# A new written order for the first two token blocks of a fused retention and expert kernel

## Chip, cores and metric

The kernel runs on one core of a Trainium2 chip. The metric is the device time of one execution in microseconds (us), as the median of several executions. Times inside an execution come from one profiled execution and are counted from the start of its span.

## What is computed

Decayed causal attention (retention) over 8 sequences of 576 positions with 8 heads of 64, then a dense expert layer with a sigmoid-approximated gelu, then a soft mixture of 8 experts with 4 slots each. All inputs and outputs are float32.

```python
ret = (q @ k.T / sqrt(64)) * gamma[h] ** (i - j)  for i >= j     # 8 x 8 x 576 x 576
x = (ret @ v), heads side by side                                # 4608 x 512
h = x @ w_in                                                     # 4608 x 2048
x = (h * sigmoid(1.702 * h)) @ w_out                             # 4608 x 512
logits = x @ phi                                                 # 4608 x 32
slot_input = softmax(logits, over tokens).T @ x                  # 32 x 512
slot_out[e] = relu(slot_input[e] @ w1[e]) @ w2[e]                # 8 experts, 4 slots each
out = softmax(logits, over slots) @ slot_out                     # 4608 x 512
```

## The kernel before

The 4608 tokens form 12 blocks of 384. A block is three steps of 128 tokens (two sequences at one chunk of 64 positions each), and nine steps make one pass over the sequence for two sequences. A step is loaded by one 1 MB transfer (`load_step`, token T), its keys are scaled on GpSimd (`scale_keys`, KN), and TensorE makes its scores (transposed), its contribution to the running state and its output (`products`, line 220: tiles Sp, St, Op). VectorE scales scores (SC), state (SS) and output (xs) out of PSUM, and the output is split into a high part (ScalarE, `x_high`, xh) and a low part (`x_low`, xl, on VectorE for steps 0 to 2 and on GpSimd from step 3 on).

A block then meets 16 weight chunks of the expert layer. One expert product (`expert_scores`, line 357, token M) is 12 matmuls of 128x384: high by high, high by low, low by high, for four pieces of the inner dimension. They read all 384 columns of the block's high and low part, so no product of a block can pass its second matmul before all three low parts are written. ScalarE makes the gelu (g), VectorE turns it (t), and when eight are turned SP shuffles them to natural order by transfers (N, 16 transfers for half a block).

The weights arrive as 64-bit words, of which the kernel makes float32: ScalarE brings the sign (ua for `w_in`, aa for `w_out` turned), VectorE shifts the low word (us, as) and joins the two (uc, ac). `w_in` is then split into high (ScalarE, h) and low (VectorE, v). Of `w_out` turned, TensorE makes `w_out @ phi` (e, line 326), which VectorE turns into Wp (ed), and the logits of a group of four chunks are products with Wp (L). Raw weights land in seven places that are used in turn (W and O tokens), so a load waits for the join or split of the piece seven before it. `slots_part` (SG, line 468) sums the natural gelus of a block into the slots.

Blocks 0 and 1 (16 + 16 expert products, M0 to M31) stand in a list of tokens, `START`, that is written out by hand. Each engine runs its own instructions in the order of this list, and nothing is reordered. From block 2 on loops write the order. Among the tokens: B0 and B3 are score products alone, P and A are products of a step with output, Q output alone, R state alone (R2: the state products of the third step). D is a product of line 558 on the loaded keys of the pack that step 3 takes over; its result is not used. G is one element on ScalarE that the first weight load waits for, so that the first three steps land ahead of the weights. K loads three small constants.

```python
    def again():
        t = ps.tile([128, NB], F32, tag="h", name="again", bufs=3)
        a = packs[0].rearrange("p c a j d -> p (c a j d)")
        pe.matmul(t, a[:, 0:128], a[:, 0:NB], start=True, stop=True)
```

Of the kernel before, what the change touches and what calls it, by code (L numbers as in the profile page):

```python
# [9 lines left out]
F32 = mybir.dt.float32  # L10
F32R = mybir.dt.float32r
I32 = mybir.dt.int32
AF = mybir.ActivationFunctionType
# [5 lines left out]
B, H, S, D = 8, 8, 576, 64  # L19
# [7 lines left out]
C = 64  # L27
NPB = S // C
NP = H // 2
NB = 384  # L30
# [16 lines left out]
PC = NP * CP  # L47

START = (
# [13 lines left out]
).split()  # L63

RAWS = 7
# [67 lines left out]
def tile_kernel(ctx, tc, qkv, w_in, w_turned, w_out, phi, w1, w2, consts, out):  # L133
    nc = tc.nc
    pe, act, dve, pool, sp = nc.tensor, nc.scalar, nc.vector, nc.gpsimd, nc.sync

    pp = ctx.enter_context(tc.tile_pool(name="pp", bufs=1))
    ps = ctx.enter_context(tc.tile_pool(name="ps", bufs=1, space=PSUM))
# [38 lines left out]
    early_raw = pm.tile([128, 6, 1024], F32, tag="nat", name="early_raw")  # L177
    packs = {g: pa.tile([128, 6, NP, NSEQ, C], F32, name=f"pack{g}", bufs=1) for g in range(2)}
# [6 lines left out]
    St, Sps, Ops, xss = {}, {}, {}, {}  # L185
# [79 lines left out]
    wt = {}  # L265
# [41 lines left out]
    def w_high(fc):  # L307
        if fc in (0, NFC - 1):
            wt[fc] = pw.tile([128, 2, NDC, 128], F32R, tag="w1", name="w", bufs=2)
        elif fc % 2:  # L310
            two = pw.tile([128, 2, 2, NDC, 128], F32R, tag="w", name="w")
            wt[fc], wt[fc + 1] = two[:, 0], two[:, 1]
        act.copy(wt[fc].rearrange("p a c f -> p a (c f)")[:, 0], raws[f"W{fc}"][0].bitcast(F32))

    def w_low(fc):
# [233 lines left out]
    def constants():  # L549
        sp.dma_start(phis.rearrange("p c s -> p (c s)"), phi)  # L550
        sp.dma_start(ident, consts[:, 0:128])
        s4 = st["s4"] = pm.tile([128, 128], F32, tag="dT", name="s4")
        sp.dma_start(s4, consts[:, _CONSTS.shape[1] - 128:])

    def again():
        t = ps.tile([128, NB], F32, tag="h", name="again", bufs=3)
        a = packs[0].rearrange("p c a j d -> p (c a j d)")
        pe.matmul(t, a[:, 0:128], a[:, 0:NB], start=True, stop=True)

    what = {  # L560
        "T": load_step,
        "W": lambda i: load_w(f"W{i}"), "O": lambda i: load_w(f"O{i}"),
        "ua": lambda i: bring_sign(f"W{i}"), "us": lambda i: shift_low(f"W{i}"),
        "uc": lambda i: join(f"W{i}", raws[f"W{i}"][0]), "h": w_high, "v": w_low,
        "aa": lambda i: bring_sign(f"O{i}"), "as": lambda i: shift_low(f"O{i}"),
        "ac": lambda i: join(f"O{i}", ring[:, i % 4]), "e": wp_product, "ed": wp_turn,
# [10 lines left out]
    def step(x):  # L577
        if x == "C":
            sp.dma_start(cs, consts[:, 128:128 + NCS])
        elif x == "K":  # L580
            constants()
        elif x == "D":
            again()
        elif x == "G":
            act.copy(early_raw[0:1, 0, 0:1], St[0][0:1, 0, 0, 0:1])
        elif x == "Z":
            dve.tensor_copy(sum4r, st.pop("s4"))
        else:
            name = x.rstrip("-0123456789")
            what[name](int(x[len(name):]))  # L590
# [230 lines left out]
    with tc.manual_schedule(engines={getattr(mybir.EngineType, e) for e in ("PE", "Activation", "DVE", "Pool", "SP")}):  # L821
        for x in START:
            step(x)
# [122 lines left out]
```

## Time and profile before

| | |
|---|---|
| median of 3 executions | 656.14 us (654.52 to 657.8) |
| the profiled execution, its own time | 653.52 us |
| its span, first to last instruction | 651.7 us |
| TensorE matmul busy in the span | 627.9 us (96%) |
| VectorE, ScalarE, GpSimd busy | 291.7, 218.4 and 80.4 us |
| first expert product of block 0 (M0) begins | 19.59 us |
| first expert product of block 1 (M16), second matmul | 68.87 us |
| first expert product of block 2, second matmul | 119.27 us |

TensorE is busy nearly all the time, so the time of the first two blocks is told by the places where it waits. The last three lines mark the ends of the stages that the change touches; the profiled execution is 2.6 us under the median of the three.

### The profile page before, as it was taken

How to read it: one execution, taken by the hardware profiler on the slowest of the kernel's cores; microseconds unless marked ns; L12 is line 12 of the kernel's file. 1: busy time of each engine (PE TensorE's matmuls, PEld its weight loads, DVE VectorE, ACT ScalarE, POOL GpSimd, SP SyncE). 2: the span in 40 equal slices, each digit the busy share in tenths (PEclk: the TensorE clock that was granted, in tenths of full speed). 3: DMA queues.
4: the chain of work that ended last, by engine and by line, in shares of the span. 5: the costliest groups of instructions: out<-in, count | busy, mean ns of one | idle time of the engine just before them, and what ended most of it. 6: DMA issues, size and time to landing. Idle time of an engine off the chain costs nothing.

```text
span 651.7 us, 19108 instructions
## 1 busy us (share of the span) xinstructions
PE 627.9 (96%) x8439; PEld 540.8 (83%) x8439; DVE 291.7 (45%) x578; ACT 218.4 (34%) x411; POOL 80.4 (12%) x72
## 2 busy tenths in 40 slices
PE   6999999999999999999999999999999999999992
PEld 6898787898989989989989979989898798874562
DVE  3999832364453443444534534544535223122042
ACT  2784432141241332412412412412414224240042
POOL 2103102111112101121111011111111100001000
PEclk9999999999999999999999999999999999999997
DMA  8987657766776647737647557467477778989998
GB/s 341 398 308 285 253 123 204 182 192 163 198 252 171 176 183 191 211 109 200 184 131 206 163 140 215 134 163 199 162 185 200 277 197 244 404 303 419 415 419 345
DMA packets 62546, 150.64 MB, mean 231 GB/s; under 512 B 8192, under 2 KB 42368, under 8 KB 53248
## 3 DMA queue, kind: packets, MB, share of 16 engines
q1 hardware_dynamic: 62464, 149.43, 71.6%
q8 instruction: 66, 1.08, 0.7%
q14 instruction: 16, 0.13, 0.1%
HBM read 101.16 MB, written 13.63 MB: 176 GB/s over the span
## 4 chain that ended last, share of the span: by engine, by line
PE 86%; DVE 5%; DMA 4%; ACT 2%; issue 1%; POOL 0%; SPq 0%; DVEq 0%; ACTq 0%
PE hp L357 56%; PE Lg L408 5%; PE Sg L468 4%; PE Sp L220 4%; PE St L220 4%; PE Op L220 3%; PE h_ps L705 2%; PE op L782 2%; PE so_ps L756 1%; DMA early_raw<-in_moe_w_in_dram 1%; PE so_ps L748 1%; DMA ring<-in_w_turned_dram 1%; DVE w L317 1%; PE tpg L390 1%; DMA pack<-in_qkv_dram 1%
## 5 line engine op out<-in xcount | busy, mean ns | idle before, releaser
L357 PE MATMUL hp<-x,w 128*128 128x384 f32 x2304 | 418.9, 339 | 1.3 <-POOL x L250 1.3
L357 PEld LDWEIGHTS hp<-x,w 128*128 128x128 f32 x2304 | 397.5, 188 | 20.0 <-issue 16.3
L383 DVE STREAM_TRANSPOSE pre<-gT 128x384 f32<-128x384 f32 x172 | 95.1, 568 | 151.0 <-ACT gT L367 149.5
L367 ACT ACTIVATE gT<-hp 128x384 f32<-128x384 f32 x188 | 90.8, 489 | 213.7 <-PE hp L357 213.3
L250 POOL TENSOR_TENSOR x<-xs,x 128x512 fp32r<-128x512 f32 x33 | 42.7, 1293 | 294.5 <-ACT x L245 294.5
L220 PE MATMUL Op<-pack 64*64 64x64 f32 x2176 | 71.9, 220 | 0.2 <-issue 0.2
L220 PEld LDWEIGHTS Op<-pack 64*64 64x64 f32 x2176 | 66.9, 135 | 0.6 <-issue 0.6
L226 POOL TENSOR_TENSOR pack<-pack,cs 128x512 f32<-128x512 f32 x32 | 34.8, 1088 | 142.0 <-DMA pack<-in_qkv_dram 126.1
L245 ACT CAST x<-xs 128x512 fp32r<-128x512 f32 x36 | 22.3, 619 | 85.8 <-DVE xs L238 85.8
L220 PE MATMUL Sp<-pack 64*64 64x64 f32 x1152 | 41.1, 222 | 6.5 <-DMA pack<-in_qkv_dram 6.5
L220 PEld LDWEIGHTS Sp<-pack 64*64 64x64 f32 x1152 | 37.7, 138 | 8.2 <-DMA pack<-in_qkv_dram 5.7
L230 DVE TENSOR_TENSOR pack<-Sp,cs 128x512 f32<-128x512 f32 x36 | 24.8, 688 | 37.8 <-PE Op L220 19.3
L220 PEld LDWEIGHTS St<-pack 64*64 64x64 f32 x1024 | 33.2, 137 | 8.0 <-issue 7.9
L220 PE MATMUL St<-pack 64*64 64x64 f32 x1024 | 37.6, 224 | 0.0
L408 PE MATMUL Lg<-gT,Wp 128*32 128x384 f32 x376 | 36.2, 493 | 0.4 <-DVE Lall L455 0.4
L468 PE MATMUL Sg<-nat,dn 128*32 128x512 f32 x264 | 30.4, 593 | 0.0
L238 DVE TENSOR_TENSOR xs<-Op,cs 128x512 f32<-128x512 f32 x36 | 24.5, 681 | 2.8 <-PE Op L220 2.8
L234 DVE TENSOR_TENSOR pack<-St,cs 128x512 f32<-128x512 f32 x32 | 21.8, 680 | 3.7 <-PE St L220 2.2
L294 ACT ACTIVATE early_raw<-early_raw 128x512 f32<-128x512 f32 x28 | 18.9, 688 | 12.6 <-DMA early_raw<-in_w_turned_dram 7.6
L468 PEld LDWEIGHTS Sg<-nat,dn 128*32 128x32 f32 x264 | 8.5, 110 | 17.0 <-issue 17.0
L294 ACT ACTIVATE ring<-ring 128x512 f32<-128x512 f32 x20 | 13.7, 683 | 23.7 <-DMA ring<-in_moe_w_out_dram 21.3
L474 DVE SCALAR_TENSOR_TENSOR acc<-acc,corr,Sg 128x512 f32<-128x512 f32 x10 | 7.5, 747 | 28.2 <-PE Sg L468 28.2
(143 smaller groups left out, 378.4 us busy)
## 6 DMA issues: line engine op xcount, KB each, us to landing
pack<-in_qkv_dram SPq DMA_DIRECT2D x36, 1024.0 KB, 5.5
nat<-pre SPq DMA_DIRECT2D x352, 96.0 KB, 2.2
wx<-in_moe_w_dram SPq DMA_DIRECT2D x20, 1024.0 KB, 10.9
ring<-in_moe_w_out_dram SPq DMA_DIRECT2D x16, 512.0 KB, 3.7
early_raw<-in_moe_w_in_dram SPq DMA_DIRECT2D x15, 512.0 KB, 5.9
early_raw<-in_w_turned_dram SPq DMA_DIRECT2D x13, 512.0 KB, 7.6
wx<-in_moe_w_dram SPq DMA_DIRECT2D x10, 512.0 KB, 9.1
out_dram<-wx SPq DMA_DIRECT2D x5, 1024.0 KB, 9.1
```

The source lines that it names most:

```text
L220: pe.matmul(o[oh, p, j, :], w[h, a, p, j], w[h, b, p, j], start=first_, stop=True, skip_group_check=True)
L226: pool.tensor_tensor(k, k, by_state(ksc[:, n % NPB, :]), op=ALU.mult)
L230: dve.tensor_tensor(packs[n][:, SC], Sps.pop(n), across(dtab), op=ALU.mult)
L238: dve.tensor_tensor(xss[g], Ops.pop(g), across(osc), op=ALU.mult)
L245: act.copy(xh[b_][:, :, i * CP:(i + 1) * CP], xss[g].rearrange("p a j c -> p a (j c)"))
L250: (eng or pool).tensor_tensor(xl[b_][:, :, cols_], xss.pop(g).rearrange("p a j c -> p a (j c)"), xh[b_][:, :, cols_], op=ALU.subtract)
L294: act.activation(upper, upper, AF.Prelu, scale=2.0 ** -112, alpha=2.0 ** 32)
L357: pe.matmul(hp, wt[fc][:, a, dc, :], b[n][:, dc, :], start=(i == 0), stop=(i == 3 * NDC - 1))
L367: act.activation(gT[n, g][:, fl, :], hps.pop((n, fc)), AF.Gelu_apprx_sigmoid)
L383: dve.transpose(pre[n, hf][:, :, :, fh, :].rearrange("p c b i -> p (c b) i"), gT[n, g][:, fl, :].rearrange("p (x j) -> p x j", j=32))
L408: pe.matmul(Lg[n][32 * fl:32 * fl + 32, :], Wp[:, g * GF + fl, :], gT[n, g][:, fl, :], start=(g == 0), stop=(g == NFC // GF - 1))
L468: pe.matmul(Sg[32 * b:32 * b + 32], dn[n][:, c, :], nv[:, 4 * b:4 * b + 4], start=(c == 0), stop=(c == NT128 - 1))
```

## The change

The list `START` is written anew for all engines. It holds the same tokens, but for the three D, which are gone together with the function `again`. R2 moves ahead of M0. G is now a gelu of one element instead of a copy. `w_high` no longer takes it that the odd one of two chunks comes first. Two lines of the list, of some forty, and the code:

```diff
-    "T0 C T1 T2 B0 KN0 SC0 R0 G SS1 P0 KN1 W0 W1 R1 SC1 T3 W2 xs0 W3 KN2 SS2 P1 xh0 W4 W5 xl0 SC2 T4 ua0 W6 xs1 Q2 D "
+    "T0 C T1 KN0 B0 SC0 R0 SS1 KN1 P0 T2 G SC1 xs0 R1 xh0 W0 P1 W1 K KN2 SS2 ua0 xl0 W2 SC2 us0 Q2 xs1 uc0 xs2 W3 xh1 "
...
-        elif fc % 2:
+        elif fc not in wt:
+            i = (fc - 1) // 2 * 2 + 1
             two = pw.tile([128, 2, 2, NDC, 128], F32R, tag="w", name="w")
-            wt[fc], wt[fc + 1] = two[:, 0], two[:, 1]
+            wt[i], wt[i + 1] = two[:, 0], two[:, 1]
...
-    def again():
-        t = ps.tile([128, NB], F32, tag="h", name="again", bufs=3)
-        a = packs[0].rearrange("p c a j d -> p (c a j d)")
-        pe.matmul(t, a[:, 0:128], a[:, 0:NB], start=True, stop=True)
...
-        elif x == "D":
-            again()
         elif x == "G":
-            act.copy(early_raw[0:1, 0, 0:1], St[0][0:1, 0, 0, 0:1])
+            act.activation(early_raw[0:1, 0, 0:1], St[0][0:1, 0, 0, 0:1], AF.Gelu_apprx_sigmoid)
```

TensorE around the first expert product, before (pack_94 is the third step, pack_92 the first and then the fourth; `again` is D, `hp` an expert product of 12):

```order
L220 MATMUL Op<-pack_94 64x64 x32
L558 MATMUL again<-pack_92 128x384 x3
L357 MATMUL hp<-x,w 128x384 x12
L220 MATMUL St<-pack_94 64x64 x16
L357 MATMUL hp<-x,w 128x384 x24
L220 MATMUL Sp<-pack_92 64x64 x16
L357 MATMUL hp<-x,w 128x384 x48
```

and now:

```order
L220 MATMUL Op<-pack_94 64x64 x32
L220 MATMUL St<-pack_94 64x64 x16
L358 MATMUL hp<-x,w 128x384 x12
L220 MATMUL Sp<-pack_92 64x64 x16
L358 MATMUL hp<-x,w 128x384 x48
```

The state products stand between the outputs of the third step and the first expert product, and the scores of the fourth step follow that product at once; four expert products follow before the next step instead of two and four.

GpSimd ahead of block 2, before (x_1431 is block 2, and xs_1405, xs_1541, xs_1655 are the outputs of steps 6, 7 and 8; pack0_92 holds the keys of step 7 and, in its second row, of step 9):

```order
L226 TENSOR_TENSOR pack0_92<-pack0_92,cs_83 128x512
L250 TENSOR_TENSOR x_1431<-xs_1405,x_1431 128x4x128
L250 TENSOR_TENSOR x_1431<-xs_1541,x_1431 128x4x128
L226 TENSOR_TENSOR pack0_92<-pack0_92,cs_83 128x512
L250 TENSOR_TENSOR x_1431<-xs_1655,x_1431 128x4x128
L226 TENSOR_TENSOR pack1_93<-pack1_93,cs_83 128x512
```

and now (x_1359 is block 2; xs_1353, xs_1531 and xs_1650 are steps 6, 7 and 8):

```order
L226 TENSOR_TENSOR pack0_92<-pack0_92,cs_83 128x512
L250 TENSOR_TENSOR x_1359<-xs_1353,x_1359 128x4x128
L250 TENSOR_TENSOR x_1359<-xs_1650,x_1359 128x4x128
L226 TENSOR_TENSOR pack0_92<-pack0_92,cs_83 128x512
L250 TENSOR_TENSOR x_1359<-xs_1531,x_1359 128x4x128
L226 TENSOR_TENSOR pack1_93<-pack1_93,cs_83 128x512
```

The low part of step 8 now stands ahead of that of step 7, with the keys of step 9 between them.

TensorE at the end of block 1, before (Lg are the logits groups L4 and L5, hp x36 is M28 to M30, Sg is SG0, and with the Sp row the products of step 8, A8, begin):

```order
L220 MATMUL Op<-pack_92 64x64 x2
L408 MATMUL Lg<-gT,Wp 32x384 x8
L357 MATMUL hp<-x,w 128x384 x36
L468 MATMUL Sg<-nat,dn 32x512 x12
L220 MATMUL Sp<-pack_92 64x64 x2
L220 MATMUL Op<-pack_93 64x64 x2
```

and now (M28, SG0, M29, then A8):

```order
L220 MATMUL Op<-pack_92 64x64 x2
L358 MATMUL hp<-x,w 128x384 x12
L469 MATMUL Sg<-nat,dn 32x512 x12
L358 MATMUL hp<-x,w 128x384 x12
L220 MATMUL Sp<-pack_92 64x64 x2
L220 MATMUL Op<-pack_93 64x64 x2
```

SG0 stands two expert products and one logits group earlier. Behind A8 stood M31 alone; now M30, L5 and M31 stand there. On ScalarE xh8, the high part of step 8, is behind g30 in both lists.

## Rows read from the trace of the kernel before

**Rows 1.** The page: TensorE's granted clock in 40 slices, tenths.

```profile
PEclk9999999999999999999999999999999999999997
```

**Rows 2.** Timeline of TensorE, start: start us, us, instruction, count, [idle before].

```profile
5.68 1.97 PE L220 MATMUL Sp<-pack 64*64 64x64 f32 x32 [5.68 <-DMA pack<-in_qkv_dram]
...
13.09 3.07 PE L220 MATMUL Op<-pack 64*64 64x64 f32 x98 [0.23 <-issue]
17.85 2.20 PE L558 MATMUL again<-pack 128*128 128x384 f32 x6 [1.69 <-DMA pack<-in_qkv_dram]
19.59 2.54 PE L357 MATMUL hp<-x,w 128*128 128x384 f32 x12
22.06 1.15 PE L220 MATMUL St<-pack 64*64 64x64 f32 x32
```

**Rows 3.** Timeline of VectorE, up to the shuffles.

```profile
14.94 0.79 DVE L298 TENSOR_SCALAR early_raw<-early_raw 128x512 int32<-128x512 int32 x2
...
18.05 1.53 DVE L250 TENSOR_TENSOR x<-xs,x 128x512 fp32r<-128x512 f32 x1
...
21.08 0.69 DVE L317 TENSOR_TENSOR w<-early_raw,w 128x512 fp32r<-128x512 f32 x1 [0.56 <-ACT w L313]
...
24.68 0.69 DVE L317 TENSOR_TENSOR w<-early_raw,w 128x512 fp32r<-128x512 f32 x1 [1.03 <-ACT w L313]
...
39.73 0.69 DVE L317 TENSOR_TENSOR w<-early_raw,w 128x512 fp32r<-128x512 f32 x1 [0.81 <-ACT w L313]
...
50.95 0.83 DVE L298 TENSOR_SCALAR early_raw<-early_raw 128x512 int32<-128x512 int32 x1 [0.36 <-DMA early_raw<-in_w_turned_dram]
...
66.17 0.65 DVE L238 TENSOR_TENSOR xs<-Op,cs 128x512 f32<-128x512 f32 x1
...
79.96 0.69 DVE L303 SCALAR_TENSOR_TENSOR ring<-early_raw 128x512 int32<-128x512 int32 x1
...
94.18 2.88 DVE L383 STREAM_TRANSPOSE pre<-gT 128x384 f32<-128x384 f32 x6 [1.23 <-DMA nat<-pre]
```

**Rows 4.** Timeline of TensorE, blocks 0 to 2.

```profile
60.46 0.85 PE L408 MATMUL Lg<-gT,Wp 128*32 128x384 f32 x8
...
68.87 6.34 PE L357 MATMUL hp<-x,w 128*128 128x384 f32 x35 [0.91 <-POOL x L250]
...
81.20 1.10 PE L326 MATMUL wps<-ring,phis 128*32 128x64 f32 x64
...
111.58 2.78 PE L468 MATMUL Sg<-nat,dn 128*32 128x512 f32 x24
...
116.32 2.54 PE L357 MATMUL hp<-x,w 128*128 128x384 f32 x13
119.27 8.42 PE L357 MATMUL hp<-x,w 128*128 128x384 f32 x47 [0.41 <-POOL x L250]
```

**Rows 5.** Windows: stretch, length, busy us of PE, PEld, DVE, ACT, POOL, clock, DMA.

```profile
19.59:25.00 5.41, 5.41 (x57) 4.96 (x56) 3.82 (x8) 5.14 (x8) 0.00 (x0) 1.00 1.02 418
...
45.00:50.00 5.00, 4.22 (x105) 3.86 (x107) 5.00 (x12) 4.33 (x9) 0.38 (x1) 1.00 0.84 317
...
65.00:70.00 5.00, 3.47 (x75) 2.65 (x74) 5.00 (x12) 1.38 (x3) 1.27 (x1) 1.00 0.82 304
```

**Rows 6.** Timeline of ScalarE.

```profile
21.78 1.28 ACT L367 ACT_TABLE_LOAD   x1
...
117.23 0.62 ACT L245 CAST x<-xs 128x512 fp32r<-128x512 f32 x1 [5.05 <-DVE xs L238]
```

**Rows 7.** Timeline of GpSimd.

```profile
17.96 1.06 POOL L226 TENSOR_TENSOR pack<-pack,cs 128x512 f32<-128x512 f32 x1 [5.28 <-DMA pack<-in_qkv_dram]
...
117.93 1.28 POOL L250 TENSOR_TENSOR x<-xs,x 128x512 fp32r<-128x512 f32 x1 [4.43 <-ACT x L245]
```

**Rows 8.** Timeline of SP's queue: the shuffles of block 0.

```profile
80.68 11.65 SPq L401 DMA_DIRECT2D nat<-pre  x16
...
95.38 11.82 SPq L401 DMA_DIRECT2D nat<-pre  x16
```

24 rows, old and new, of the table START are left out of this document.

## The prediction

> **What bounds the kernel now.** I read the page first, for the engine at its limit, then TensorE's timeline for the places where it waits, then the timelines of the engines that it waits for. TensorE runs at full clock through the whole span but its end [rows 1], and almost without a pause from the first expert product (M0) to the end, so a new order can give only what TensorE loses in waits before block 2, plus whatever work moves into a wait. Those waits are few. M0 is listed at 19.59 us, but the six rows of D run from 17.85 for 2.20 us, so it gets going only at about 20.05 [rows 2]. The stretch from 45 to 50 us has 0.8 us without a matmul, where the scores of step 5 wait for their load, and that from 65 to 70 us has 1.5 us [rows 5], most of it ahead of M16's second matmul at 68.87, which waits for GpSimd's low part of step 5 [rows 4]. A last wait, 0.4 us by the row, stands ahead of 119.27: block 2's second matmul waits for the low part of step 8 [rows 4]. I use two marks of the trace, 68.87 (block 1) and 119.27 (block 2), and count everything against them. Behind the second the order of the program is the same, so a shift there should reach the end.
>
> **The change, part by part.**
>
> *R2 and D.* The outputs of step 2 end at 13.09 + 3.07 = 16.16 [rows 2]. R2, 32 rows in 1.15 us [rows 2], runs right behind them, in time that was a wait. It leaves the path behind M0, which gives 1.1 us. D's removal matters for M0's start: M0 needs the low part of step 2 (xl2) and W0's low part. Before, xl2 took 1.53 us instead of about 0.69 [rows 3], because GpSimd scaled the keys of step 3 from 17.96 on [rows 7]. The load of step 3 (T3) now stands behind K, W2 and W3, 1.24 MB more, which at 418 GB/s [rows 5] is 3.0 us, so it lands at about 20.8 instead of 17.8 and the collision moves onto a later VectorE instruction at the same 0.84 us. Behind 16.16 come the scaling of the output (0.69), its high part on ScalarE (0.62 [rows 6]), xl2 (0.69), and W0's low part, which now stands behind xl2 (0.6): 16.9, 17.6, 18.3, 18.9. Two of M0's matmuls can run ahead of the last of these, so M0 in effect runs from 18.7: 1.35 us earlier. The scores of step 3 directly behind M0 then wait about 0.3 us for T3.
>
> *G.* ScalarE loads its table for the first gelu at 21.78 in 1.28 us [rows 6]; with G as a gelu the load before the first data remains and this one goes. The 1.28 us are part of the gaps that VectorE has behind 21 us (next part), and are not counted again.
>
> *VectorE up to step 5's output.* This engine sets 68.87: the scaling of step 5's output (xs5) starts at 66.17 [rows 3], in a stretch in which VectorE is full while TensorE waits [rows 5]: VectorE is working off its list. The new list has five items fewer ahead of xs5 (as8, as9, t8, t9, t10): three turns of 0.48 (2.88 for six) and two shifts of 0.35, 2.1 us [rows 3]. VectorE's four gaps, 0.56, 1.03, 0.81 and 0.36, together 2.8 us [rows 3], were waits for a split on ScalarE or for a load that came late; in the new order I find each operand there when its turn comes. New waits at the start (xs2 stands behind TensorE, xl2 behind ScalarE) cost 0.5 us more than before. Collisions with GpSimd are four in both. So xs5 starts at 66.17 - 2.1 - 2.8 + 0.5 = 61.8, and 2.7 us later, as before (66.17 to 68.87), M16 may pass its second matmul: 64.5.
>
> *TensorE to the same place.* From 20.05 to 68.87 are 48.8 us. R2's 1.1 and the waits of 0.8 and 1.5 leave 45.4; step 5's load now stands ahead of O2 and its scores no longer wait. From 18.7 this gives 64.1; with the 0.3 for T3, and 0.3 where I see M4 catch up with W4's low part, 64.7. The two paths meet within their errors, and I take 64.7: 4.2 us earlier than 68.87.
>
> *What is given back: SG0.* It needs the 32 shuffles of block 0, which SP issues in 11.65 and 11.82 us [rows 8], pace set by SP, and which start when the last join of `w_out` pieces (ac15) is done: before, 79.96 + 0.69, and the first shuffle at 80.68 [rows 3, 8]. In the new list ac15 stands behind e6's turn and two turns. TensorE reaches e6's end at 64.7 + (81.20 - 68.87) - 2.15 (one expert product fewer ahead, 8.42 for 47 rows) + 0.55 (half of 1.10) = 75.4 [rows 4]; VectorE needs 0.2 + 2 x 0.48 + 0.69 = 1.85 more, so ac15 ends at 77.3. Then 11.65 + 0.4 for T8 + 11.82, and 1.85 for the last landing (the turn that waits for the first half starts at 94.18, the first half's issue ended at 92.33 [rows 3, 8]): block 0 is in natural order at 103.05. TensorE reaches SG0 at 64.7 + (111.58 - 68.87) less M29, M30 and L5 (2 x 2.15 + 0.7), 102.4 [rows 4]. SG0 waits 0.6 us where it had more than 2 us of slack.
>
> *What is given back: the low parts of block 2.* SG0 with the switch to A8 and A8 itself took 111.58 to 116.32, 4.75 us [rows 4]; with M29 A8 ends at 103.05 + 4.75 + 2.15 = 109.95. xh8 is behind g30, which waits for M30: 2.2 + 0.15 + 0.4 + 0.62 [rows 6], then xl8 1.28, the keys of step 9 1.04 and xl7 1.28 [rows 7]: 7.0 us, so block 2's second matmul can run at 117.0. TensorE alone would be there after M30, L5 and M31, 5.4 us. Before, only 2.95 us lay between A8's end and 119.27. SP has no new wait of weight: T10 moves ahead of block 1's first shuffle and waits for A8, but T9 ahead of it lands in time.
>
> **Sum.** 117.0 against 119.27 is 2.3 us earlier. Against the profiled execution that is 653.52 - 2.3 = 651.2; the median of the runs shown lies 2.6 us above it, and 656.14 - 2.3 = **653.8 us**. The 4.2 us won by M16 are in part spent on SG0 (0.6) and on the order of GpSimd's low parts (1.4 more than the old wait). 0.5%, about what a measurement of this kernel can tell from no change, is 3.3 us.
>
> **Rivals.**
>
> *TensorE alone decides.* If g30 and the low parts do not hold block 2 and the shuffles are in time, block 2 comes 49.65 us behind M16 as before (68.87 to the end of M31, 116.32 + 2.15 [rows 4]): 114.4 with its second matmul, 4.8 us earlier, 651.3 us. For it: before, such waits were short. Against: xl7 stands in GpSimd's list behind xl8, and xl8 needs g30's engine; that is in the order. Chance 0.19.
>
> *VectorE wins nothing, and the shuffles turn it into a loss.* Everything behind hangs on ac15: block 2's second matmul is 39.7 us behind it (117.0 - 77.3). The new order breaks even where ac15 ends at 79.5, and the old trace has 80.65. If xs5 starts no earlier than 66.17, since the gaps that I take away come back at other splits, M16 stays at 68.87, ac15 at 81.4, and block 2 at 121.1: 1.9 us later, **658.0 us**. For it: VectorE is full in the stretches from 45 to 50 and 65 to 70 us [rows 5], and each split waits on two engines. Against: 2.1 us of its work really stand behind xs5. Chance 0.14, of which a third over 0.5%.
>
> *The clock.* [...] Chance 0.05.
>
> **How the numbers follow.** Forecast 0.59 (652.9 to 655.3: ac15 0.8 us earlier or later, and more where small waits add up), TensorE alone 0.19, VectorE wins nothing 0.14, clock 0.05, something else 0.03. Faster by over 0.5%: TensorE alone and 0.07 of the forecast's lower end, 0.26. Slower by over 0.5%: 0.05. Within: 0.69. The range reaches from just under TensorE alone, 651.1, to 657.6, short of the second rival's time; about 2 in 10 lie outside.
>
> **What would show it.** Right: R2 ends near 17.3; M0 begins near 18.7; no table load between the start and the softmax; xs5 starts near 62 with VectorE without gaps over 0.5 us from 19 to 60; M16 passes its second matmul near 64.7; the first shuffle goes out at 77.3; SG0 waits a little for a transfer; block 2's second matmul waits for GpSimd near 117.0, and the tail from there to the end is as long as before. [...]

## The result and the profile after

The new order is slower: 658.62 us (657.67 to 660.46, 10 runs) against 656.01 (652.22 to 658.19, 10 runs), a ratio of 1.0053 with a 95% interval of [1.0037, 1.0069]. The prediction was 653.8, and its range ended at 657.6. The two profiled executions lie further apart than the medians, 659.14 against 653.52: before was caught 2.5 us below its median. So lengths are read from the traces, the verdict from the ratios.

| us | before | predicted | after |
|---|---|---|---|
| M0 in effect | 20.05 | 18.7 | 18.65 |
| scores of step 3 begin | | 20.8 | 23.86 |
| scaling of step 5's output (xs5) | 66.17 | 61.8 | 67.68 |
| M16, second matmul | 68.87 | 64.7 | 70.43 |
| first shuffle | 80.68 | 77.3 | 83.50 |
| turned block 0 (SG0) begins | 111.58 | 102.4 | 109.59 |
| block 2, second matmul | 119.27 | 117.0 | 124.67 |

The first row flatters the change: before, M0's first matmul ran beside the last D, and the rows of M0 end at 19.59 + 2.54 = 22.13 and at 18.65 + 2.54 = 21.19, 0.94 us apart. From block 2 on nothing changed: its second matmul is 532.5 us ahead of the span's end before and 532.7 after. TensorE's timeline of after, at the places of [rows 2, 4] (start, length, engine, line, operation, tiles, count, idle time ahead and who ended it):

```profile
18.65 2.54 PE L358 MATMUL hp<-x,w 128*128 128x384 f32 x12
...
23.86 1.97 PE L220 MATMUL Sp<-pack 64*64 64x64 f32 x32 [2.67 <-DMA pack<-in_qkv_dram]
25.76 10.63 PE L358 MATMUL hp<-x,w 128*128 128x384 f32 x48
...
70.43 4.25 PE L358 MATMUL hp<-x,w 128*128 128x384 f32 x23 [0.50 <-POOL x L250]
...
109.59 3.82 PE L469 MATMUL Sg<-nat,dn 128*32 128x512 f32 x24
...
117.64 2.35 PE L358 MATMUL hp<-x,w 128*128 128x384 f32 x12
...
124.67 3.56 PE L358 MATMUL hp<-x,w 128*128 128x384 f32 x19 [1.42 <-POOL x L250]
```

M0 starts where it was put. Behind it the scores of step 3 wait 2.67 us for their load, and the 32 score matmuls, 1.15 us in before (27.50), take 1.97. The windows around it say why (stretch, length, busy us of PE, PEld, DVE, ACT, POOL, granted clock, DMA share, GB/s):

```profile
10.00:23.40 13.40, 9.44 (x284) 8.43 (x276) 10.63 (x20) 5.94 (x11) 1.47 (x2) 1.00 0.88 323
23.40:30.20 6.80, 6.34 (x46) 6.25 (x47) 5.74 (x12) 4.74 (x9) 1.08 (x1) 0.50 1.02 419
```

The granted clock is 0.50 of full for 6.8 us behind that wait. It looks like the culprit. VectorE's timeline up to step 5, to be held against [rows 3], says otherwise:

```profile
21.23 0.69 DVE L303 SCALAR_TENSOR_TENSOR early_raw<-early_raw 128x512 int32<-128x512 int32 x1 [0.82 <-ACT early_raw L294]
...
25.12 0.43 DVE L298 TENSOR_SCALAR early_raw<-early_raw 128x512 int32<-128x512 int32 x1 [1.06 <-DMA early_raw<-in_moe_w_in_dram]
...
35.96 0.69 DVE L303 SCALAR_TENSOR_TENSOR early_raw<-early_raw 128x512 int32<-128x512 int32 x1 [1.59 <-ACT early_raw L294]
...
67.68 0.68 DVE L238 TENSOR_TENSOR xs<-Op,cs 128x512 f32<-128x512 f32 x1
```

The gaps of which the prediction said that none would be left are eight here, 5.8 us in all (these three and 0.52, 0.42, 0.53, 0.39, 0.48), where before had four with 2.8. Five wait for a weight's load, three for ScalarE. The longest, 1.59 us, goes back to TensorE: ahead of the sign for that join, ScalarE has a gelu that waited as long for an expert product.

```profile
34.34 0.49 ACT L368 ACTIVATE gT<-hp 128x384 f32<-128x384 f32 x1 [1.59 <-PE hp L358]
```

Taken off 67.68, the 5.8 us of gaps leave 61.9, the forecast's 61.8. By that subtraction the moved work was counted rightly, and the gaps are what was wrong. What SP issues at the start shows where they are:

```profile
10.45 1.85 SPq L280 DMA_DIRECT2D early_raw<-in_moe_w_in_dram  x2
12.34 0.44 SPq L551 DMA_DIRECT2D phis<-in_moe_phi_dram  x1
...
13.78 0.91 SPq L280 DMA_DIRECT2D early_raw<-in_moe_w_in_dram  x2
14.81 0.65 SPq L183 DMA_DIRECT2D pack<-in_qkv_dram  x1
```

Before, the first two weights went out at 9.79 in 0.80 us and step 3 at 10.87. The three constants now hold SP from 12.34 to 13.73 us, for 0.19 MB. The first weights write over the place that G uses, so they wait for G, and ScalarE's row of G shows for whom G now waits, the scaling of the state (SS1) on VectorE (before, G ran at 9.62):

```profile
10.27 0.16 ACT L579 ACTIVATE early_raw<-St 1x1 f32<-1x1 f32 x1 [8.25 <-DVE pack L234]
```

The DMA rate, last column of the windows, of after and then of before:

```profile
10.00:12.00 2.00, 1.78 (x84) 1.67 (x78) 1.51 (x4) 0.16 (x1) 0.56 (x2) 1.00 0.66 221
12.00:14.00 2.00, 1.74 (x85) 1.60 (x87) 1.91 (x4) 0.62 (x1) 0.90 (x1) 1.00 0.78 252
```

```profile
10.00:12.00 2.00, 2.00 (x96) 1.94 (x91) 1.72 (x4) 0.00 (x0) 0.54 (x2) 1.00 0.90 315
12.00:14.00 2.00, 1.77 (x89) 1.63 (x82) 1.91 (x4) 0.62 (x1) 0.68 (x1) 1.00 1.09 428
```

The next two windows, up to 18 us, have 287 and 294 against 399 and 377, so from 10 to 18 us after moves 2.11 MB and before 3.04. The missing 0.93 MB are 2.2 us at the 418 GB/s of [rows 5]: the load of step 3, put at 20.8 for the 1.24 MB ahead of it, would be there at 23.0, and the row has 23.86.

### The profile page after: what moved, and what is told of

Read it like the earlier page. It is cut to its first block, busy times and chain, and to the rows that moved or that the text cites. A ratio compares the mean times of both kernels' runs of the same rounds, so it can differ in the third digit from the quotient of the medians.

```text
span 657.3 us, 19091 instructions
## 1 busy us (share of the span) xinstructions
PE 631.4 (96%) x8433; PEld 541.7 (82%) x8433; DVE 292.0 (44%) x578; ACT 216.6 (33%) x410; POOL 80.1 (12%) x72
## 4 chain that ended last, share of the span: by engine, by line
PE 81%; DMA 4%; issue 4%; DVE 4%; SPq 2%; ACT 2%; POOL 1%; DVEq 0%; POOLq 0%; ACTq 0%
PE hp L358 53%; PE Lg L409 5%; PE Sg L469 4%; PE Sp L220 4%; PE St L220 4%; PE h_ps L699 2%; PE Op L220 2%; DMA pack<-in_qkv_dram 2%; DMA early_raw<-in_w_turned_dram 2%; PE op L776 2%; SPq L402 2%; PE so_ps L750 1%; PE so_ps L742 1%; POOL x L250 1%; PE tpg L391 1%
```

## Experiments

**How far a mark can be trusted.** Traces of kernels with the same list up to M16 differ: with the old one M16's second matmul is at 68.87, 68.99, 69.66 and 70.43 (71.32 and 70.45 without D), with the new one at 70.43, 70.42, 70.37 and 68.07. The length from there to block 2's second matmul is steadier. Marks of one trace under 2 us apart decide nothing in the first half. So the new first half isn't shown to be slower than the old one; it has lost the lead that was forecast.

| kernel | M16 | first shuffle | SG0 begins | block 2 | M16 to block 2 | time | ratio [95%] |
|---|---|---|---|---|---|---|---|
| before | 68.87 | 80.68 | 111.58 | 119.27 | 50.4 | 656.01 | 1 |
| after | 70.43 | 83.50 | 109.59 | 124.67 | 54.2 | 658.62 | 1.0053 [1.0037, 1.0069] |
| e1_fill | 70.37 | 83.98 | 109.78 | 125.58 | 55.2 | 659.85 | 1.0064 [1.0038, 1.0091] |
| e2_t3 | 67.14 | 80.14 | 106.09 | 121.62 | 54.5 | 657.65 | 1.0041 [1.0020, 1.0062] |
| e3_xl7 | 70.42 | 83.49 | 109.44 | 123.71 | 53.3 | 657.52 | 1.0034 [1.0020, 1.0048] |
| e4_noD | 71.32 | 84.70 | 115.59 | 123.28 | 52.0 | 654.87 | 0.9994 [0.9978, 1.0010] |
| e5_stream | 66.43 | 80.05 | 106.01 | 121.39 | 55.0 | 657.31 | 1.0010 [0.9988, 1.0033] |
| e6_sg0 | 68.07 | 81.86 | 109.58 | 122.72 | 54.6 | 658.28 | 1.0040 [1.0016, 1.0064] |
| e7_gelu | 68.99 | 80.91 | 111.78 | 119.48 | 50.5 | 655.73 | 0.9994 [0.9968, 1.0020] |
| e8_all | 67.99 | 81.91 | 110.27 | 121.80 | 53.8 | 654.97 | 0.9980 [0.9952, 1.0007] |
| e9_r2 | 70.45 | 82.25 | 113.16 | 120.85 | 50.4 | 655.71 | 1.0014 [0.9999, 1.0029] |
| e10_g | 68.41 | 81.45 | 108.13 | 123.10 | 54.7 | 656.56 | 1.0017 [1.0001, 1.0033] |
| h2_second | 69.66 | 85.10 | 111.08 | 126.63 | 57.0 | 660.92 | 1.0095 [1.0073, 1.0116] |
| h3_first | 67.48 | 79.82 | 110.71 | 118.40 | 50.9 | 653.53 | 0.9977 [0.9960, 0.9994] |
| s1_split | 70.43 | 82.60 | 114.18 | 121.88 | 51.4 | 656.06 | 1.0016 [0.9996, 1.0035] |

Each time is the median of 10 to 12 executions (5 of e1_fill, 6 of h2_second). Each ratio is to runs of before on the same chip, whose medians were 654.58 to 656.01.

**Is it the clock, or TensorE's wait for step 3?** e1_fill puts four products on loaded data into that wait:

```
-... ua4 M0 uc3 us4 ...
+... ua4 M0 D D D D uc3 us4 ...
```

> The changed kernel with four products like D (results unused, on loaded keys of step 1) between M0 and the scores of step 3, so that TensorE has work while it waits for step 3's load. [...] Rival: the slow clock costs little, since the expert products behind it wait for split weights anyway; then M4 ends near 36 with TensorE waiting at full clock, and the time stays at 658.6 us.

```profile
23.40:30.20 6.80, 6.29 (x61) 5.75 (x60) 4.96 (x11) 4.49 (x8) 1.04 (x1) 1.00 0.97 363
```

The granted clock stays full (1.00). xs5 starts at 67.61 instead of 67.68, M16 stands at 70.37 instead of 70.43, and the kernel is no faster, 659.85 us, where the theory, by which the slow stretch costs about 3 us, had 655.7. TensorE's 6.8 slow microseconds cost nothing here, since VectorE sets M16. VectorE's wait of 1.59 us is gone, but its waits for loads are longer: 1.84 instead of 1.06 behind 23 us, then 1.36, 0.86 and 1.20. The clock also fell in e4_noD (0.50 from 20.3 to 23.7 us) and in h3_first (8 tenths in the second of the page's 40 slices, 16.3 to 32.6 us), which are not slower than before.

**Is it the order of the loads?** e2_t3 puts the load of step 3 behind W1 and the constants K behind W10, and the sign and the join of W1 ahead of W2's; e5_stream also puts G ahead of the state's scaling (SS1), and e10_g does that alone:

```
e10_g  -... SS1 KN1 P0 T2 G SC1 ...   +... G SS1 KN1 P0 T2 SC1 ...
e2_t3  -... W1 K KN2 ... us2 T3 ...   +... W1 T3 KN2 ... W10 K A3 ...
e5_stream: both
```

> The new kernel with G ahead of the state's sum, as in the kernel before, nothing else. Theory (its wait for the sum holds the first two weight loads by 0.66 us, and all loads behind them): W0 and W1 land 0.7 to 1.5 us earlier, near 14.0 and 15.3, the load of step 3 near 22.8 instead of 23.7, the scaling of step 5's output near 67.0, block 2 near 124.0, 658.0 us. Rival (the loads of the constants and their place set the pace, not G): W2 and step 3 land as before within 0.3 us and nothing moves, 658.6 us.

> The changed kernel with step 3's load ahead of W2 and the constants (K) behind W10, as they stood before, and with W1's sign and join ahead of those of W2. Theory A: the place of that load is the cause of the loss. [...] Rival: M1 to M4 wait for their split weights, whose loads now come later, for 2 us or more, the clock falls again, and the time is 657 us or more.

> The changed kernel with the early transfers as they stood before: G ahead of the second step's state scaling, step 3's load ahead of K and W2, K behind W10, and W1's sign and join ahead of those of W2. Theory B (formed from the runs so far): the path to block 1 goes through the raw weights and VectorE, and the changed kernel's transfers run at about two thirds of their rate from 10 to 18 us, since G waits for a VectorE instruction (first weight load issued at 10.45 instead of 9.79 us) and SP issues the three small constants next. Without both, W0 lands near 14.0, step 3 near 17.9 and W4 near 22.4 instead of 25.1; xs5 starts near 63 instead of 67.7, M16's second matmul runs near 66, and the time is 655.5 us. The e2 run, which has all but G's place, had M16 at 67.1. Rival: VectorE is behind for another reason than the transfers (its own order); M16 stays at 67 or later, and the time is as in e2, 657.6 us.

In e10_g the first weights go out at 9.72 in 0.80 us, the rate from 10 to 18 us is 323 GB/s instead of 264, and step 3's scores start at 21.79. The time goes from 1.0053 to 1.0017 of before, two thirds of the loss for one token, and the intervals don't overlap. e2_t3's 1.0041 can't be told from after; its theory had block 1 near 66 and 654 us, and M16 came at 67.14, the time at 657.65. e6_sg0, whose list is that of after up to there, lends support: in its execution the first weights happened to go out at 10.15 in 0.80 us, the rate was 319, and M16 came at 68.07. The same windows of after and e5_stream:

```profile
10.00:18.00 8.00, 6.70 (x270) 6.31 (x263) 6.57 (x12) 2.92 (x6) 1.47 (x2) 1.00 0.79 264
```

```profile
10.00:18.00 8.00, 6.38 (x241) 5.89 (x231) 7.14 (x12) 3.10 (x6) 1.32 (x3) 1.00 0.97 363
```

All nine traces with the new first half fall in line. The three that move 2.10 to 2.12 MB in this window (after, e1_fill, e3_xl7) have xs5 at 67.61 to 67.68; the six that move 2.46 to 2.97 MB have it at 63.67 to 65.62. With e5_stream's list xs5 and M16 come within 2 us of the prediction:

```profile
63.67 0.68 DVE L238 TENSOR_TENSOR xs<-Op,cs 128x512 f32<-128x512 f32 x1
```

```profile
65.86 4.31 PE L358 MATMUL hp<-x,w 128*128 128x384 f32 x21
```

M16 runs without a wait, its second matmul at 66.43. So the first half lost most of its lead to the start's transfers. But block 2 comes 55.0 us later, at 121.39, and the time doesn't beat before.

**Does the second half lose time by itself?** h2_second has the old list up to M16 and the new one behind, h3_first e5_stream's list up to M16 and the old one behind (without D). Tokens that the second list has ahead of M16 and the first behind it stand ahead of it in the mixture (as11 and aa12 in h2_second, seven in h3_first):

```
h2_second: tokens of before up to M16, then the rest in the order of after
h3_first:  tokens of e5_stream up to M16, then the rest in the order of before
```

> The old order up to M16 (block 1), and from there the new one: it asks whether the second half of the new order loses time on its own. Theory (it does: low parts of step 7 behind those of step 8, the turned block's matmuls ahead of M29, more changes between kinds of matmul): M16 passes its second matmul at 68.9 us as in the kernel before, block 2's second matmul comes 53.5 to 54.5 us later instead of 50.4, at about 123, and the time is about 3.5 us over the kernel before, 659.5. Rival (the second half is no worse, the 54.2 us of the new kernel came from what its first half had left undone): block 2 near 119.5, 656.

> The new order up to M16 with the start's transfers mended as in e5_stream (G ahead of the state's sum, the load of step 3 behind W1, the constants behind W10), and from M16 on the old order, without D. Theory (the first half is worth its 2.4 us once the loads flow, and the old second half keeps them): M16's second matmul near 66.5 us, the first shuffle near 78.3, block 2's second matmul near 116.9, 653.6 us. Rival (the lead ends at the shuffles or at the low parts of steps 6 to 8 whatever the order): M16 near 66.5 all the same, block 2 at 118 to 119.5, 655 to 656 us, no different from the kernel before.

The second half does it: 57.0 us with the old first half, even more than in after, and the slowest kernel of all; 50.9 with the mended new first half and the old second one. More than half of h2_second's surplus of 2.8 us over after is a wait of TensorE for a turn on VectorE. That turn stands behind a shift that waits for a raw piece of `w_out`, so this part belongs to the mixture:

```profile
76.24 0.84 PE L409 MATMUL Lg<-gT,Wp 128*32 128x384 f32 x4 [1.56 <-DVE Wp L331]
```

```profile
75.61 0.43 DVE L298 TENSOR_SCALAR early_raw<-early_raw 128x512 int32<-128x512 int32 x1 [2.96 <-DMA early_raw<-in_w_turned_dram]
```

h3_first is the only version that is faster than before beyond its interval, by 1.5 us; it is one of thirteen, and its interval ends at 0.9994. Its time is the theory's (653.6), but block 2 stands where the rival had it (118 to 119.5). Its rows at the two places:

```profile
110.71 2.78 PE L469 MATMUL Sg<-nat,dn 128*32 128x512 f32 x24
115.45 2.54 PE L358 MATMUL hp<-x,w 128*128 128x384 f32 x13
118.40 1.83 PE L358 MATMUL hp<-x,w 128*128 128x384 f32 x9 [0.41 <-POOL x L250]
```

SG0 takes 2.78 us, not 3.82, and block 2 waits as little as in [rows 4].

**Where the second half's 3.8 us are (54.2 against 50.4).** The low parts first. GpSimd in after, then in e3_xl7, where the low part of step 7 stands ahead of that of step 8 (xl7 before xl8):

```profile
121.10 1.29 POOL L250 TENSOR_TENSOR x<-xs,x 128x512 fp32r<-128x512 f32 x1 [19.37 <-ACT x L245]
122.34 1.04 POOL L226 TENSOR_TENSOR pack<-pack,cs 128x512 f32<-128x512 f32 x1
123.34 1.27 POOL L250 TENSOR_TENSOR x<-xs,x 128x512 fp32r<-128x512 f32 x1
```

```profile
117.43 1.27 POOL L250 TENSOR_TENSOR x<-xs,x 128x512 fp32r<-128x512 f32 x1 [15.83 <-ACT x L245]
121.73 1.29 POOL L250 TENSOR_TENSOR x<-xs,x 128x512 fp32r<-128x512 f32 x1 [3.04 <-ACT x L245]
```

> The changed kernel with the low part of step 7 ahead of that of step 8 on GpSimd, as it stood before. Theory A: block 2's second matmul waits 1.4 us for GpSimd because step 7's low part is written last, 7.0 us behind A8's end; now it would be ready 4.7 us behind A8's end, ahead of TensorE's own 5.4, so the wait goes: block 2 at 123.3 instead of 124.7, 657.3 us. Rival: another wait for the same place ends there (the keys of step 9, a shuffle), and the time stays at 658.6 us.

Low part of step 8, keys, low part of step 7 in a row, as read from the order; with step 7 first the wait of 1.42 at block 2 is gone, and M16 to block 2 is 0.9 shorter; the time, 1.0034, can't be told from after's. Then SG0. Its row takes 3.82 us in after, and in e1_fill it is split by a wait for a shuffle:

```profile
111.55 2.77 PE L469 MATMUL Sg<-nat,dn 128*32 128x512 f32 x20 [0.72 <-DMA nat<-pre]
```

In e6_sg0 it is moved behind M29, so that the last shuffle has landed:

> The changed kernel with SG0 behind M29 instead of M28 on TensorE; the other engines as they are. Theory A: SG0 meets the last shuffles, whose last landing is held up to 110.2 us by the load of step 9, and takes 3.7 instead of 2.7 us; one expert product later they have landed, SG0 takes 2.8, and block 2 comes 1.0 us earlier: 657.6 us. Rival: the wait moves to step 8's products, which need VectorE behind the same shuffle, and the time stays at 658.6 us.

```profile
109.58 2.78 PE L469 MATMUL Sg<-nat,dn 128*32 128x512 f32 x24
...
122.72 1.49 PE L358 MATMUL hp<-x,w 128*128 128x384 f32 x7 [1.43 <-POOL x L250]
```

SG0 is back at 2.78, but the length to block 2 is 54.6, not shorter: with no expert product between SG0 and A8, A8 waits for VectorE's copy of SG0's result and for the scores' scaling behind it (0.55 and 0.25 us). Third, up to SG0 after takes 39.16 us from M16, and before 42.71 less M29, M30 and L5 (5.0), 37.71: 1.45 more. s1_split takes before's pairs of small matmuls apart:

```
-M17 M18 L1 | M19 M20 e6 e7 M21 M22 L2 L3 M23
+M17 L1 M18 | M19 e6 M20 e7 M21 L2 M22 L3 M23
```

> The kernel before with its pairs of small matmuls between M16 and the end of block 1 taken apart: L1 ahead of M18, e6 and e7 each behind one expert product, L2 and L3 too. The same matmuls, four more groups of expert products. Theory (each further change between kinds of matmul costs TensorE about 0.1 to 0.2 us: an expert product between other matmuls takes 2.28 us in the new kernel where half of two in a row is 2.18, eight matmuls of an L alone 0.78 where half of sixteen is 0.72): the turned block 0 begins 0.8 to 1.0 us later behind M16 than the 42.7 us of the kernel before, and the time is 0.5 to 1 us up, since a part falls into the old wait for the low part of step 8. Rival (the changes are free, and the 1.45 us that the new order loses there are small waits for other engines): 42.7 us within 0.2, and no change in time.

```profile
81.01 0.65 PE L326 MATMUL wps<-ring,phis 128*32 128x64 f32 x32
81.60 2.35 PE L357 MATMUL hp<-x,w 128*128 128x384 f32 x12
83.88 0.65 PE L326 MATMUL wps<-ring,phis 128*32 128x64 f32 x32
84.46 2.35 PE L357 MATMUL hp<-x,w 128*128 128x384 f32 x12
86.75 0.85 PE L408 MATMUL Lg<-gT,Wp 128*32 128x384 f32 x8
```

SG0 starts 43.75 us behind M16 instead of 42.71, with no wait in between: 1.04 for three more groups of expert products and three more of small matmuls (the expectation's "four" is a miscount). The time can't be told from before. An expert product alone takes 2.28 from start to start (81.60 to 83.88), and half of two in a row 2.18. After has the same pairs apart, with A6 beside L2. By the starts of its rows that is 1.04 us (expert products 0.61, L's 0.30, e's 0.13); another 0.46 lie around the three small matmuls ahead of M27, which waits for an activation. So 1.45 us of the 3.8 lie ahead of SG0, 1.04 in it and 1.0 in the wait at block 2 (1.42 against 0.41). Taking the wait away shortens the way to block 2 (e3_xl7), taking SG0's part away doesn't (e6_sg0), and the 1.45 us were taken away in no run.

**All mends in the new order.** e8_all is e5_stream with SG0 behind M29 and xl7 first:

> The e5 version with SG0 behind M29 and step 7's low part ahead of step 8's. If the three losses (transfers at the start, SG0 on the last shuffles, the order of the low parts) are separate and are all of the loss, block 2's second matmul runs near 116.5, and the time is 653 us, 2 us under the kernel before. If one of them only covers another, it stays at 655 us or more.

M16 to block 2 is 53.8, and the wait at M27, 0.21 us in after, is 1.25. It is for an activation on ScalarE behind step 6's high part and a table load (1.28 us at 100.38 in after, at the same place); the high part waits for VectorE, whose turn ahead of step 6's output waited 1.21 us for a shuffle:

```profile
100.82 2.35 PE L358 MATMUL hp<-x,w 128*128 128x384 f32 x12 [1.25 <-ACT gT L368]
```

The time, 0.9980 [0.9952, 1.0007], is clear of after's interval but can't be told from before. Block 2 is 2.5 us later than in the trace of before, which was caught 2.5 us below its median.

**The named parts alone, in the old list.** e4_noD takes D out, e7_gelu makes G a gelu, e9_r2 puts R2 ahead of M0 and takes D out:

```
e4_noD   -... xs2 Q2 D D D us0 ...      +... xs2 Q2 us0 ...   (three D)
e7_gelu  -act.copy(early_raw[..], St[0][..])   +act.activation(.., AF.Gelu_apprx_sigmoid)
e9_r2    -M0 us2 h1 KN3 ua3 v1 R2 g0    +R2 M0 us2 h1 KN3 ua3 v1 g0   (no D)
```

> The kernel before without the three products D, and nothing else. Theory A (the clock falls where TensorE waits long): without D TensorE waits from 16.2 to about 19.6 us, where the low part of step 2 is late, 3.4 us; the clock falls for some 7 us from about 19 on, and the time is 2 to 3 us longer than before, 658.5 us. Rival: D only stood in the way (M0 begins 0.3 us earlier without it), the clock stays full, and the time is as before or 0.3 us shorter, 655.7 us.

> The kernel before with G as a gelu instead of a copy, and nothing else: one table load of 1.28 us at M0's gelu goes. Theory A: ScalarE is on VectorE's path there (VectorE waits 1.0 us for W2's high part at 24.7), so VectorE and block 1 come about 1 us earlier: M16's second matmul near 67.9 instead of 68.9, 654.1 us against 655.1. Rival: the gap comes back at the next split, and nothing can be measured, 655.1 us.

> The kernel before with R2 ahead of M0 and without D, nothing else moved: the change's name by itself. Theory (VectorE and its splits set M16): M0 begins near 18.7 instead of 20.05, M16's second matmul stays within 0.7 us of 68.87, and the time stays within 0.7 us of the kernel before. Rival (TensorE's work ahead of M16 counts): M16 is 1.1 to 1.4 us earlier and so is the end, 654.7. A dip of the granted clock behind the wait for M0, as in e4_noD, would take about 1 us more on TensorE.

None moves the time by what can be told. In e4_noD the clock is at 0.50 for 3.4 us from 20.3, and its mean over the execution is 0.990 against 0.995 in before; the time is the same. In e9_r2, whose clock is at 8 tenths in the second slice of its page, M0 doesn't even start earlier: VectorE's low part of step 2 collides with GpSimd's keys of step 3 (18.07 for 1.23 us) as in [rows 3, 7], takes 1.53 us where that of step 1 at 17.11 took 0.68, ends at 19.84, and M0 begins at 20.06.

```profile
18.31 1.53 DVE L250 TENSOR_TENSOR x<-xs,x 128x512 fp32r<-128x512 f32 x1
```

So what after's M0 gained came from the late load of step 3, which moved that collision away. In e2_t3, e5_stream, h3_first and e8_all, where this load comes early again, M0 starts at 19.51 to 19.83.

## Why the prediction was wrong, point by point

Block 2's second matmul missed its forecast by 7.7 us (124.67 against 117.0). Of these 5.7 were there at M16 (70.43 against 64.7) and 1.9 came behind it (54.2 us against 52.3).

- *R2, D, M0 at 18.7*: right in place, 18.65, and for the reason given, the collision that the late load moves away (two low parts take 1.46 us together at 17.06 in after). By the ends of M0 the gain is 0.94 us, not 1.35, and it was worth nothing, since VectorE sets M16; in e4_noD and e9_r2, too, taking D out and moving R2 left the time where it was.
- *The load of step 3 at 20.8*: wrong by some 3 us. The step counted the bytes of K, W2 and W3 at the full rate. It left out that SP takes 1.4 us to issue the constants of K, that G's new place holds the first weights (0.66 us) and that the rate from 10 to 18 us falls to 221, 252, 287 and 294 GB/s in windows of 2 us, where before had 315, 428, 399 and 377. I had looked at G only for its table load.
- *The table load*: gone as said (after has none between 0.73 and 95.52 us), and worth nothing measurable (e7_gelu).
- *VectorE without gaps, xs5 at 61.8*: the step that failed. The 2.1 us of moved items are real, but instead of losing gaps of 2.8 us it has 5.8, so in these two traces xs5 starts 1.5 us later than before, not 4.4 earlier. "I find each operand there when its turn comes" took the order of the loads for their landing. With the transfers mended the row stands at 63.67 to 65.23 in three of the traces (e5_stream, h3_first, e8_all) and M16 at 66.4 to 68.0. What keeps it 2 to 3.4 us short of the forecast is gaps again, 2.2 to 3.0 us in each, at weight loads (1.19 us at 49.30 in h3_first) and behind ScalarE (0.96 at 32.34 in e5_stream); no run takes them apart.
- *First shuffle 12.6 us behind M16*: right, 13.07. *Block 2 39.7 behind ac15*: 41.2 from the first shuffle.
- *SG0's wait, 0.6*: mis-sized, 1.04 (3.82 against 2.78). SP's rows show the shuffles at the pace of [rows 8], and the load of step 9 (T9) right behind them; that it slowed the last shuffle is argued, not tried.

```profile
83.50 11.81 SPq L402 DMA_DIRECT2D nat<-pre  x16
...
95.99 11.03 SPq L402 DMA_DIRECT2D nat<-pre  x16
107.47 10.61 SPq L183 DMA_DIRECT2D pack<-in_qkv_dram  x2
```

- *TensorE's way to SG0*: the sum took 42.71 less three terms; the 1.45 us of more changes and one small wait weren't in it (s1_split).
- *7.0 us from A8 to block 2*: right to 0.03 (117.64 to 124.67), and the wait for GpSimd came as said. It is 1.42 us against 0.41 before, so 1.0 more and not the sum's 1.4; e3_xl7 takes it away.
- *The rivals*: the second one, that VectorE wins nothing and the shuffles turn it into a loss, is what happened, by its own link from ac15 to block 2. That its 658.0 us is close to 658.62 is in part luck: it had block 2 at 121.1, and the row has 124.67, counted from a trace of before that lay 2.5 us below the median. It was held at 0.14 because "2.1 us of its work really stand behind"; the price of starting the transfers late was on no side of the scale. TensorE alone did not decide, since block 2 waits for GpSimd. The rival on the clock, that TensorE's pause without D lowers it, was the author's estimate; no row of before shows it. It was half right: in after the clock fell to 0.50, behind the 2.67 us wait for step 3, not where D had been, and filling that wait gave nothing back.

## What to carry to other kernels

Where a list orders all engines at once, cost first what it does to the transfers of the first microseconds: a dummy instruction whose buffer a load will write over is a wait for that load (G at 10.27, the load at 10.45), and a rate from a stretch in which the queue was full can't be used where it isn't (418 GB/s in [rows 5], 264 from 10 to 18 us in after). Look for an engine that sets a mark before pricing idle time of another; TensorE's pause and slow clock were free here because VectorE was late anyway (xs5 at 67.68 with them, at 67.61 in e1_fill without the slow clock). Where two halves of an order are changed at once, join each to the old other half: here the old second half behind the mended new first half was the one version clear of before's time, by 0.23%, close to what can be told.

## Unexpected on the hardware

- The granted clock fell to 0.50 behind a wait of 2.67 us for 6.8 us (after) and for 3.4 us in e4_noD, where TensorE had 1.44 and 0.71 us without a matmul around M0. In e2_t3 the windows from 20 to 24 us have 0.52 and 0.63, and h3_first and e9_r2 have 8 tenths in the second of the page's 40 slices. The pause of 1.7 us in [rows 2] left it at 1.00. The length of the pause alone doesn't tell: it fell around the 1.44 and 0.71 us in e4_noD and stayed up behind one of 2.30 us in e6_sg0, where the 32 score matmuls behind the pause took 1.15 us.
- Changing between kinds of matmul cost TensorE time in s1_split: an expert product that stands alone takes 2.28 us from start to start where half of two in a row takes 2.18, and eight matmuls of an L alone 0.78 (86.75 to 87.53) where half of sixteen in before takes 0.72 (86.59 to 88.02). Over the stretch up to SG0 that is 0.63 for the products and 0.40 for the small groups, together 1.04 us to rounding.
- Two weight loads took SP 0.80 to 0.81 us to issue where they went out at 9.72 to 10.15 us (e10_g, before, h2_second, h3_first, e6_sg0) and 1.60 to 1.85 where they went out at 10.45 to 10.58 (after, e1_fill, e2_t3, e3_xl7). G waited for the same instruction in these four and in e6_sg0, which took 0.80. Why they differ isn't settled.
